# A DeltaNet recurrence with a SwiGLU FFN: one stream of units, inversions by pairs, and a fixed order

## The chip, the cores and the metric

The kernel runs on one core of a Trainium2 chip. The metric is the device time of one execution in microseconds (us), the median of several runs. A core has five engines that run side by side, each with its own queue of instructions: TensorE (matmuls, PE in the profile; its weight loads are PEld), VectorE (DVE), ScalarE (ACT), GpSimd (POOL) and SyncE (SP), which here only starts DMA transfers. TensorE writes to PSUM, and VectorE and ScalarE move results from there to SBUF.

## The reference: what is computed

Two layers follow each other. The first is a DeltaNet: for each of 4 batches and 8 heads a state of 48x48 is carried over 768 positions.

```python
k_n = k / (np.linalg.norm(k, axis=-1, keepdims=True) + 1e-06)
for t in range(S):                                   # S = 768
    y[:, :, t] = einsum('bhd,bhde->bhe', q[:, :, t], state)
    v_old = einsum('bhde,bhd->bhe', state, k_n[:, :, t])
    state += beta[:, :, t, None, None] * einsum('bhd,bhe->bhde', k_n[:, :, t], v[:, :, t] - v_old)
```

The second is an FFN on the 3072 tokens of width 384 (8 heads x 48), with 1536 inner columns:

```python
xn = x / sqrt(mean(x * x) + 1e-06) * rms_g
out = (silu(xn @ w_gate) * (xn @ w_val)) @ w_out
```

The kernel doesn't walk over positions. It cuts the 768 positions into 6 chunks of 128 and calls one chunk of one batch a **unit**; there are 24, and unit n is chunk n // 4 of batch n % 4. Inside a unit the positions depend on each other through a triangular system, which is inverted in blocks of 32 positions (and the blocks are then joined by matmuls). Between chunks only the state of a batch is passed on. All data are float32; the weights arrive as 64-bit floats and are converted on the chip.

## The kernel before

A unit goes through these steps. `prepare` transposes q and k on TensorE, forms all products of keys and queries (`score`), and writes the 32x32 diagonal blocks out to DRAM, from where they come back with one block on each partition (`gather`):

```python
def gather(n):
    c, b = divmod(n, B)                      # B = 4
    ...
    for a in range(NBLK):
        dma(out=gds[c][...], in_=gp[b][W * a : W * (a + 1), :, o : o + W])
    if b == B - 1:
        nc.sync.dma_start(out=gblk, in_=gds.pop(c))

def prepare(n):
    norm_k(n, square_k(n, nc.scalar))
    yield 4
    transpose(n, qpad[n % 2], Q0)
    ...
    yield 3
    transpose(n, kpad[n % NK], K0)
    yield 2
    score(n, crossed((0, slice(0, 3)), (1, slice(1, 4))), both)
    yield 1
    gather(n)
```

With 4 units x 8 heads x 4 blocks, the 128 blocks of a whole chunk lie on the 128 partitions and are inverted together, in 31 steps of two VectorE instructions:

```python
def invert(c, dt):
    clear_ttb()
    scale_beta(c)
    turn_beta(c)                             # p_nb on TensorE, nbeta on VectorE
    for b in range(B):
        scale_v(B * c + b)
    yield dt
    for i in range(W - 1):                   # W = 32
        ...
        nc.vector.scalar_tensor_tensor(out=tmp, in0=gblk[...], scalar=nbeta[:, i : i + 1],
                                       in1=ttb[...], op0=ALU.mult, op1=ALU.mult)
        nc.vector.tensor_tensor(out=to, in0=to, in1=tmp, op=ALU.add)
        yield dt
    nc.sync.dma_start(out=td, in_=ttb)
    nc.vector.tensor_tensor(out=gblk, in0=ttb..., in1=nbeta..., op=ALU.mult)
    nc.sync.dma_start(out=nd, in_=gblk)
    ...                                      # td and nd are read back as tt[b] and ne
```

The recurrence of a chunk is a small pipeline over its 4 units. Stage `corner` joins the 32-blocks of one unit (p_v) and of the one before it (p_w); `inner` forms z, u and x of three neighbouring units in one loop of small matmuls; `outer` applies the state of one unit (p_k), forms the output of another (p_y) and updates its state (p_s):

```python
for s in range(-3, B + 2):                   # once per chunk, from chunk 1 on
    inner(s, s - 1, s + 1)                   # z of s, u of s-1, x of s+1, if they exist
    yield dt
    outer(s + 1, s - 1)
    yield dt
    if s + 2 in units or s + 3 in units:
        corner(s + 3, s + 2)
    if s - 1 in units:
        ys[s - 1] = scale(*ys[s - 1])
    if s - 2 in units:
        transpose_y(B * c + s - 2, ys.pop(s - 2))      # p_xt, then xt for the FFN
    yield dt
```

The FFN takes 256 tokens at a time, in 12 tiles f of 128 inner columns:

```python
for f in range(f0, f1):
    for i in range(2):                       # gate, value
        ... # matmuls p_gv[:, i] <- wgv_sb, xt
        yield 1
    nc.scalar.activation(out=sil, in_=p_gv[:, 0], func=ACTF.Silu)
    nc.vector.tensor_tensor(out=h_f, in0=sil, in1=p_gv[:, 1], op=ALU.mult)
    if last is not None:
        leave(f - 1, last)                   # matmuls p_o <- h_f, wo_sb
        yield 1
    last = h_f
```

All parts are generators on one plan. `at(time, part)` starts a part, a `yield dt` puts its next piece dt later, and the pieces are written to the program by their plan time. A unit of plan time stands for one stretch of FFN matmuls. Up to plan time 60 the program is issued just as it is written; after that a scheduler of the framework may move instructions.

```python
CYC = 3 * FT * B // 2                        # 72
for c in range(1, NCH):
    t0 = CYC * c
    for b in range(B):
        at((8 if c == 1 else t0 - 76) + 4.5 * b, prepare(B * c + b))
    at(35 if c == 1 else t0 - 49, invert(c, 0.62))
    at(*((57, recur(c, 0.7)) if c == 1 else (t0 - 25, recur(c, 1.2))))
    for g in range(B // 2):
        at(t0 + CYC // 2 * g, ffn(B // 2 * c + g, 0, FT))
with tc.manual_schedule():
    first = recur(0, 1.2, begin())
    ...
    run_plan(60)
run_plan()
```

Of the kernel before, what the change touches and what calls it, by code (L numbers as in the profile page):

```python
# [21 lines left out]
W = 32  # L22
# [6 lines left out]
def kernel(  # L29
# [36 lines left out]
    NK = B + 1  # L66
# [20 lines left out]
    g_sb = const.tile([128, KT], FP32, name="g_sb")  # L87

# [22 lines left out]
    vraw, later = {}, []  # L111

# [136 lines left out]
    def weights():  # L249
# [37 lines left out]
        bits_pool.close()  # L287

# [36 lines left out]
    def scale_beta(c):  # L325
        nrm = norms[c]
        nc.vector.tensor_scalar_add(nrm, nrm, 1e-6)
        krec = work.tile([128, BH], FP32, name="krec", bufs=1)
        nc.vector.reciprocal(krec, nrm)
        for i in range(2):  # L330
            nc.vector.tensor_tensor(out=beta_t[:, c], in0=beta_t[:, c], in1=krec, op=ALU.mult)

    def turn_beta(c):
        p_nb = ps_delta([128, W], "p_nb")
        for a in range(NBLK):
            wa = slice(W * a, W * (a + 1))
            nc.tensor.matmul(p_nb[wa], beta_t[wa, c], ident[wa, wa], skip_group_check=True)
        nc.vector.tensor_scalar(out=nbeta, in0=p_nb, scalar1=-1.0, scalar2=None, op0=ALU.mult)

# [10 lines left out]
    def transpose(n, pad, place):  # L350
# [11 lines left out]
        nc.scalar.copy(kqt[n % B][:, :, place::2], p_t)  # L362


    def score(n, groups, evacuate):
        b = n % B
# [31 lines left out]
    def gather(n):  # L398
        c, b = divmod(n, B)
        dma = nc.scalar.dma_start  # L400
        if b == 0:
            gds[c] = dram.tile([128, W, W], FP32, name="gd")
        for a in range(NBLK):
            o = diagonal(a)
            dma(
                out=gds[c][a * BH + b * H : a * BH + (b + 1) * H].rearrange("h r j -> r h j"),
                in_=gp[b][W * a : W * (a + 1), :, o : o + W],
            )
        if b == B - 1:
            nc.sync.dma_start(out=gblk, in_=gds.pop(c))  # L410


    def gather_two(n):
        if n == 0:
            gds[0] = dram.tile([128, W, W], FP32, name="gd")
# [15 lines left out]
    def prepare(n):  # L431
        norm_k(n, square_k(n, nc.scalar))
        yield 4
        transpose(n, qpad[n % 2], Q0)
        if n + 2 < NU:
            load_q(n + 2)
        yield 3
        transpose(n, kpad[n % NK], K0)
        yield 2
        score(n, crossed((0, slice(0, 3)), (1, slice(1, 4))), both)  # L440
        yield 1
        gather(n)
# [45 lines left out]
    def clear_ttb():  # L488
        nc.gpsimd.memset(ttb, 0.0)  # L489
        nc.gpsimd.memset(ttb.rearrange("p j i -> p (j i)")[:, 0 : W * W : W + 1], 1.0)  # L490


    def invert_halves():
# [25 lines left out]
        td = dram.tile([128, W, W], FP32, name="td")  # L519
        nc.sync.dma_start(out=td, in_=ttb)  # L520

        nd = dram.tile([128, W, W], FP32, name="nd")
# [21 lines left out]
    def invert(c, dt):  # L544
        clear_ttb()
        scale_beta(c)
        turn_beta(c)
        for b in range(B):
            scale_v(B * c + b)
        yield dt  # L550
        for i in range(W - 1):
            n = W - 1 - i
            shape = [128, i + 1, n]
            tmp_b = work.tile([128, W * W // 4], FP32, name="tmp")
            tmp = tmp_b[:, 0 : n * (i + 1)].rearrange("p (k j) -> p k j", j=n)
            nc.vector.scalar_tensor_tensor(  # L556
                out=tmp,
                in0=gblk[:, i, None, i + 1 :].to_broadcast(shape),
                scalar=nbeta[:, i : i + 1],
                in1=ttb[:, 0 : i + 1, i : i + 1].to_broadcast(shape),  # L560
# [3 lines left out]
            to = ttb[:, 0 : i + 1, i + 1 :]  # L564
            nc.vector.tensor_tensor(out=to, in0=to, in1=tmp, op=ALU.add)  # L565
            yield dt
        td = dram.tile([128, W, W], FP32, name="td")
        nc.sync.dma_start(out=td, in_=ttb)

        nd = dram.tile([128, W, W], FP32, name="nd")  # L570
        nc.vector.tensor_tensor(
            out=gblk,
            in0=ttb.rearrange("p s m -> p m s"),
            in1=nbeta[:, :, None].to_broadcast([128, W, W]),
            op=ALU.mult,
        )
        nc.sync.dma_start(out=nd, in_=gblk)
        for b in range(B):
            for a in range(NBLK):
                o = W * (a % 2)  # L580
                nc.sync.dma_start(
                    out=tt[b][W * a : W * (a + 1), :, o : o + W],
                    in_=td[a * BH + b * H : a * BH + (b + 1) * H].rearrange("h r j -> r h j"),
                )
            for a in (0, 2):
                nc.sync.dma_start(
                    out=ne[W * a : W * (a + 1), b * H : (b + 1) * H],
                    in_=nd[a * BH + b * H : a * BH + (b + 1) * H].rearrange("h r j -> r h j"),
                )
        yield dt  # L590

    xts = {}
# [9 lines left out]
    def recur(c, dt, inverses=None):  # L604
        units = range(B)
        vss, x2s, p_zs, us = {}, {}, {}, {}

        def over_d(b, p):
            return beta_t[p, c, b * H : (b + 1) * H, None].to_broadcast([HC, H, D])


        def corner(b_v, b_w):
            p_v = ps_delta([128, H, W], "p_v") if b_v in units else None
            p_w = ps_delta([128, H, W], "p_w") if b_w in units else None
            for h in range(H):
                for a in (0, 2):
                    wa, wb = (slice(W * x, W * (x + 1)) for x in (a, a + 1))
                    if b_v in units:
                        o = diagonal(a)
                        nc.tensor.matmul(  # L620
                            p_v[wa, h],
                            gp[b_v][wb, h, o : o + W],
                            tt[b_v][wb, h, W:HC],
                            skip_group_check=True,
                        )
                    if b_w in units:
                        nc.tensor.matmul(  # L627
                            p_w[wa, h],
                            left(b_w)[wa, h, 0:W],
                            vss[b_w][wa, h],  # L630
                            skip_group_check=True,
                        )
            if b_v in units:
                if c == 0:
                    turn(b_v)
                vss[b_v] = work.tile([128, H, W], FP32, name="vs")
            for a in (0, 2):
                wa = slice(W * a, W * (a + 1))
                if b_v in units:
                    nc.scalar.copy(vss[b_v][wa], p_v[wa])  # L640
                if b_w in units:
                    nc.scalar.copy(tt[b_w][wa, :, W:HC], p_w[wa])


        def left(b):
            if c == 0:
                return ne_2[:, b % 2 * H : (b % 2 + 1) * H]
            return ne[:, b * H : (b + 1) * H]


        def turn(b):
            turned = work.tile([128, W * W // 4], FP32, name="tmp").rearrange(
                "p (h j) -> p h j", j=W
            )
            nc.vector.transpose(out=turned, in_=tt[b][:, :, 0:W])
            for a in (0, 2):
                wa = slice(W * a, W * (a + 1))
                nc.vector.scalar_tensor_tensor(
                    out=left(b)[wa, :, 0:W],
                    in0=turned[wa],  # L660
                    scalar=-1.0,
                    in1=beta_t[wa, c, b * H : (b + 1) * H, None].to_broadcast([W, H, W]),
                    op0=ALU.mult,
                    op1=ALU.mult,
# [4 lines left out]
        def halves(b):  # L669
            p_v = ps_delta([128, H, 2, SW], "p_vh")  # L670
            for h in range(H):
                for p, place in ((lo, K0), (hi, K1)):
                    nc.tensor.matmul(
                        p_v[p, h],
                        gp[b][p, h, HC * place : HC * (place + 1)],
                        tt[b][p, h].rearrange("p (x j) -> p x j", x=2)[:, :, SW:W],
                        skip_group_check=True,
                    )
            v_h = work.tile([128, H, W], FP32, name="vs")
            nc.scalar.copy(v_h.rearrange("p h (x j) -> p h x j", x=2), p_v)  # L680
            yield
            p_w = ps_delta([128, H, 2, SW], "p_wh")
            for h in range(H):
                for p in (lo, hi):
                    nc.tensor.matmul(
                        p_w[p, h].rearrange("p x j -> p (x j)"),
                        left(b)[p, h],
                        v_h[p, h],
                        skip_group_check=True,
                    )  # L690
            for a in range(NBLK):
                up, at = slice(W * a, W * a + SW), W * (a % 2) + SW
                to = tt[b][up, :, at : at + SW]
                if b % 2:
                    nc.scalar.copy(to, p_w[up, :, a % 2])
                else:
                    nc.vector.tensor_copy(out=to, in_=p_w[up, :, a % 2])
            yield


        def outer(b_k, b_y):
            if b_k in units and c > 0:
                p_k = ps_delta([128, H, D], "p_k")
                product(p_k, kqt[b_k], (K0, K1), state[b_k], True)
                r = vraw[B * c + b_k]
# [397 lines left out]
```

## Time and profile before

| what | value |
|---|---|
| time, median of 3 runs | 864.64 us (863.49 to 866.26) |
| span of the profiled execution | 866.4 us |
| TensorE busy | 832.2 us, 96% |
| VectorE busy | 411.9 us, 48% |
| ScalarE busy | 251.7 us, 29% |
| GpSimd busy | 107.0 us, 12% |
| mean granted TensorE clock | 0.982 |
| first FFN matmul | at 65.7 us |
| period of a chunk in the steady part | 132.0 us (564.2 to 696.3 us, the same point of two chunks) |

The profile names each group of instructions by the line of the kernel, the engine, and out<-in by the names of the program. The matmuls are pipelined, so the time of a stage is best read from the start of one group to the start of the next in the timeline. The FFN's lines are 958 (p_gv) and 945 (p_o); line 969 is h_f, the product that p_o needs. Lines 556 and 565 are the two instructions of an inversion's step. Lines 771, 780 and 789 are z, u and x in `inner`, 753 p_k and the state's part of p_y, 373 the scores, 387 their masks, 405 and 410 the two transfers of the gather. In the slices of the page each digit is the busy share of 1/40 of the span, in tenths.

### The profile page before, as it was taken

The page shows a single profiled execution, that of the slowest core. Times are in us where ns is not written, and L with a number is a line of the kernel's source. Part 1 is how long each engine was busy: PE and PEld are TensorE (multiplying, and loading weights), DVE is VectorE, ACT ScalarE, POOL GpSimd, SP SyncE. Part 2 cuts the span into 40 slices and gives each one's busy share as a digit, 9 for nine tenths or more (in the row PEclk, how much of TensorE's full clock was granted, in tenths as well). Part 3 has the DMA queues.
Part 4 walks back from the last instruction along what each step waited for, and adds up shares of the span by engine and source line. Part 5 has one row for each costly group of instructions (what it writes and reads, how often), then busy time and mean ns, then how long its engine had stood idle before and what let it go on. Part 6 is the DMA issues. An engine that isn't in the chain of part 4 may idle for free.

```text
span 866.4 us, 20251 instructions
## 1 busy us (share of the span) xinstructions
PE 832.2 (96%) x8640; PEld 638.7 (74%) x8640; DVE 411.9 (48%) x1000; ACT 251.7 (29%) x655; POOL 107.0 (12%) x146
## 2 busy tenths in 40 slices
PE   7898979689999999999999999999999999999998
PEld 6576757467887777877777887777777777777776
DVE  7869969791443761343661442671333581220100
ACT  5344446003334113244113244112334112220101
POOL 6012433100230000230000230000130000000000
PEclk9969999899999999999999999999999999999999
DMA  8846345104221131221121222122121122000000
GB/s 152 231 99 211 121 122 144 31 24 90 48 62 34 32 84 28 48 62 32 31 83 32 43 61 37 31 78 38 39 57 19 31 71 35 2 20 0 19 1 18
DMA packets 152058, 52.01 MB, mean 60 GB/s; under 512 B 143616, under 2 KB 146688, under 8 KB 151968
## 3 DMA queue, kind: packets, MB, share of 16 engines
q1 hardware_dynamic: 124816, 36.95, 18.5%
q0 software_dynamic: 2080, 10.23, 3.5%
q10 hardware_dynamic: 25072, 3.54, 2.3%
q8 instruction: 68, 1.11, 0.5%
q14 instruction: 22, 0.18, 0.1%
HBM read 36.54 MB, written 14.16 MB: 59 GB/s over the span
## 4 chain that ended last, share of the span: by engine, by line
PE 79%; DVE 15%; issue 2%; ACT 2%; DMA 1%; POOL 1%; SPq 0%; DVEq 0%; ACTq 0%; POOLq 0%
PE p_gv L958 38%; PE p_o L945 18%; DVE tmp L556 4%; DVE ttb L565 3%; PE p_g L373 3%; PE p_y L715 3%; PE p_z L771 2%; PE p_t L357 2%; PE p_k L753 2%; PE p_y L753 2%; PE p_z L780 1%; PE p_x L789 1%; PE p_v L620 1%; PE p_w L627 1%; DVE h_f L969 1%
## 5 line engine op out<-in xcount | busy, mean ns | idle before, releaser
L958 PE MATMUL p_gv<-xt,wgv_sb 128*128 128x256 f32 x1728 | 416.1, 386 | 1.3 <-DVE xt L929 0.7
L958 PEld LDWEIGHTS p_gv<-xt,wgv_sb 128*128 128x128 f32 x1728 | 321.5, 191 | 66.0 <-issue 4.3
L945 PE MATMUL p_o<-wo_sb,h_f 128*128 128x384 f32 x576 | 217.7, 502 | 9.0 <-DVE h_f L969 9.0
L969 DVE TENSOR_TENSOR h_f<-sil,p_gv 128x256 f32<-128x256 f32 x144 | 60.2, 418 | 247.3 <-ACT sil L967 247.2
L967 ACT ACTIVATE sil<-p_gv 128x256 f32<-128x256 f32 x144 | 55.1, 383 | 335.8 <-PE p_gv L958 314.4
L945 PEld LDWEIGHTS p_o<-wo_sb,h_f 128*128 128x128 f32 x576 | 105.0, 192 | 61.2 <-DVE h_f L969 13.8
L556 DVE SCALAR_TENSOR_TENSOR tmp<-gblk,nbeta,ttb 128x31 f32<-128x31 f32 (+15 forms) x155 | 62.7, 405 | 4.7
L387 DVE TENSOR_TENSOR gp<-p_g,mask 64x128 f32<-64x128 f32 (+1 forms) x160 | 37.9, 277 | 43.2 <-ACT gp L383 38.7
L565 DVE TENSOR_TENSOR ttb<-ttb,tmp 128x31 f32<-128x31 f32 (+15 forms) x155 | 53.0, 342 | 4.9
L320 POOL TENSOR_TENSOR knrm<-ksum,half 128x8 f32<-128x8 f32 x24 | 41.8, 1741 | 71.0 <-DVE ksum L319 70.8
L914 POOL TENSOR_SCALAR ms<-ms 128x1 f32<-128x1 f32 x24 | 5.3, 221 | 312.0 <-ACT y L906 311.7
L362 ACT COPY kqt<-p_t 128x512 f32<-128x512 f32 x48 | 28.1, 585 | 24.9 <-PE p_t L357 24.2
L489 POOL MEMSET ttb<- 128x1024 f32 x6 | 5.7, 954 | 228.9 <-DMA td<-ttb 228.9
L771 PEld LDWEIGHTS p_z<-v_raw,tt 64*64 64x64 f32 x768 | 26.0, 142 | 9.2 <-issue 7.2
L373 PE MATMUL p_g<-kqt 64*64 64x192 f32 x640 | 31.7, 330 | 0.9 <-ACT gp L383 0.9
L640 ACT COPY vs<-p_v 32x256 f32<-32x256 f32 x48 | 17.4, 362 | 44.4 <-PE p_w L627 23.2
L780 PE MATMUL p_z<-u,x 64*64 64x48 f32 x384 | 28.8, 227 | 0.7 <-DVE u L801 0.6
L789 PE MATMUL p_x<-tt,gp 64*64 64x64 f32 x384 | 29.0, 229 | 0.2 <-issue 0.2
L771 PE MATMUL p_z<-v_raw,tt 64*64 64x48 f32 x768 | 29.2, 227 | 0.0
L373 PEld LDWEIGHTS p_g<-kqt 64*64 64x64 f32 x640 | 23.1, 132 | 8.1 <-issue 5.3
L715 PE MATMUL p_y<-u,gp 128*64 128x48 f32 x768 | 27.6, 228 | 0.0
L780 PEld LDWEIGHTS p_z<-u,x 64*64 64x64 f32 x384 | 25.7, 142 | 2.4 <-issue 1.3
(117 smaller groups left out, 784.1 us busy)
## 6 DMA issues: line engine op xcount, KB each, us to landing
kpad<-in_k_dram SPq DMA_DIRECT2D x24, 192.0 KB, 2.9
qpad<-in_q_dram SPq DMA_DIRECT2D x24, 192.0 KB, 2.9
v_raw<-in_v_dram SPq DMA_DIRECT2D x24, 192.0 KB, 2.9
out_dram<-o_sb SPq DMA_DIRECT2D x24, 192.0 KB, 1.9
gblk<-gd SPq DMA_DIRECT2D x6, 512.0 KB, 3.3
td<-ttb SPq DMA_DIRECT2D x6, 512.0 KB, 2.6
raw<-in_moe_w_val_dram POOLq DMA_DIRECT2D x8, 384.0 KB, 4.3
raw<-in_moe_w_out_dram POOLq DMA_DIRECT2D x8, 384.0 KB, 4.3
```

Of the source, the lines that this page charges most:

```text
L320: nc.gpsimd.tensor_tensor(out=norms[c][:, b * H : (b + 1) * H], in0=ksum, in1=half, op=ALU.pow)
L373: nc.tensor.matmul(to, pair[d, K1 if i else K0], pair[d, places], skip_group_check=True)
L387: nc.vector.tensor_tensor(out=to[p, :, place], in0=p_g[p, :, place], in1=mask[p, i, None].to_broadcast([p.stop, 2, HC]), op=ALU.mult,)
L556: nc.vector.scalar_tensor_tensor(out=tmp, in0=gblk[:, i, None, i + 1 :].to_broadcast(shape), scalar=nbeta[:, i : i + 1], in1=ttb[:, 0 : i ...
L565: nc.vector.tensor_tensor(out=to, in0=to, in1=tmp, op=ALU.add)
L715: nc.tensor.matmul(p_y[p, h], gp[b_y][:, h, HC * place : HC * (place + 1)], u[:, h], start=(c == 0 and h == 0), stop=True, skip_group_chec ...
L771: nc.tensor.matmul(p_zs[b_z][p, h], tt[b_z][p, h], r[p, h], start=(h == 0), stop=(p is lo), skip_group_check=True,)
L780: nc.tensor.matmul(p_zs[b_u][hi, h], x2s[b_u][:, h], us[b_u][lo, h], start=False, stop=True, skip_group_check=True,)
L945: nc.tensor.matmul(p_o[i], h_f[:, i * C : (i + 1) * C], wo_sb[:, f], start=(f == f0), stop=(f == f1 - 1),)
L958: nc.tensor.matmul(p_gv[:, i], wgv_sb[:, i * KT + t, f * 128 : (f + 1) * 128], xt[:, t], start=(t == 0), stop=(t == KT - 1),)
L967: nc.scalar.activation(out=sil, in_=p_gv[:, 0], func=ACTF.Silu)
L969: nc.vector.tensor_tensor(out=h_f, in0=sil, in1=p_gv[:, 1], op=ALU.mult)
```

## The change

The ends of the recurrence between chunks go: from unit 4 on, one slot per unit takes the next unit in, so that `corner` and `inner` always work on full neighbours, across the border of a chunk too. For that, units can't be inverted by chunks any more: from chunk 2 on they are inverted in pairs, each on 64 of the 128 partitions, in time for their slots. Keys, kqt and gp get two more buffers where needed (they lie where the weights were converted before). u of the second half gets a PSUM tile of its own and is added on VectorE. `scale_beta` moves from the start of the inversion to the end of the last `prepare`. The Silu is written right after the gate and value matmuls. The whole program is issued in the order in which the plan writes it; no scheduler moves anything.

The diff, cut to its core (cuts marked by a line of dots):

```diff
-    NK = B + 1
+    NK = B + 2
...
+    def place_of(n):
+        return n % B if n < 2 * B else (n - B) % NK
...
+    def turn_two(g):
+        c, own = betas(g, 2)
+        p = group(g, 2)
+        apart = work.tile([128, NBLK, 2 * H], FP32, name="apart", bufs=1)
+        nc.vector.tensor_tensor(out=apart, in0=beta_t[...], in1=in_block[...], op=ALU.mult)
+        p_nb = ps_delta([128, W], "p_nb")
+        nc.tensor.matmul(p_nb[p], apart.rearrange("p a h -> p (a h)"), of_block, skip_group_check=True)
+        nc.vector.tensor_scalar(out=nbeta[p], in0=p_nb[p], scalar1=-1.0, scalar2=None, op0=ALU.mult)
...
-        if b == B - 1:
-            nc.sync.dma_start(out=gblk, in_=gds.pop(c))
+        if i == size - 1:
+            nc.sync.dma_start(out=gblk[group(n // size, size)], in_=gds.pop(n // size))
...
-    def prepare(n):
+    def prepare(n, size, dts):
...
-        yield 1
-        gather(n)
+        yield dts[3]
+        gather(n, size)
+        if n % size == size - 1:
+            scale_beta(n // size, size)
...
-    def invert(c, dt):
-        clear_ttb()
-        scale_beta(c)
-        turn_beta(c)
-        for b in range(B):
-            scale_v(B * c + b)
+    def invert(g, size, dt):
+        p = group(g, size)
+        np = size * NBLK * H
+        clear_ttb(p)
+        if size == B:
+            turn_beta(g)
+            for n in range(B * g, B * (g + 1)):
+                scale_v(n)
+        else:
+            turn_two(g)
         yield dt
         for i in range(W - 1):
             n = W - 1 - i
-            shape = [128, i + 1, n]
+            shape = [np, i + 1, n]
...
+        if have(n_u):
+            u = us[n_u][hi]
...
+                nc.vector.tensor_tensor(out=tmp_b[hi], in0=p_u[hi], in1=over_d(n_u, hi), op=ALU.mult)
+                nc.vector.tensor_tensor(out=u, in0=u, in1=tmp_b[hi], op=ALU.add)
...
-        for s in range(-3, B + 2):
-            inner(s, s - 1, s + 1)
...
+    def slot(j, dts):
+        v, z, y = (n if B <= n < NU else None for n in (j, j - 1, j - 2))
+        if have(v) and v >= 2 * B:
+            scale_v(v)
+        if have(v) or have(z):
+            corner(v, z)
+        yield dts[0]
+        inner(z, y, z)
+        yield dts[1]
+        outer(v, y)
+        reload()
+        yield dts[2]
+        if have(y):
+            scaled = scale(*ys.pop(y))
+            yield dts[3]
+            transpose_y(y, scaled)
...
+                if i == 1:
+                    sil = work.tile([128, TOK], FP32, name="sil")
+                    nc.scalar.activation(out=sil, in_=p_gv[:, 0], func=ACTF.Silu)
                 yield 1
-            sil = work.tile([128, TOK], FP32, name="sil")
-            nc.scalar.activation(out=sil, in_=p_gv[:, 0], func=ACTF.Silu)
...
-    for c in range(1, NCH):
-        t0 = CYC * c
-        for b in range(B):
-            at((8 if c == 1 else t0 - 76) + 4.5 * b, prepare(B * c + b))
-        at(35 if c == 1 else t0 - 49, invert(c, 0.62))
-        at(*((57, recur(c, 0.7)) if c == 1 else (t0 - 25, recur(c, 1.2))))
+    for b in range(B):
+        at(8 + 4.5 * b, prepare(B + b, B, (4, 3, 2, 1)))
+    at(35, invert(1, B, 0.62))
+    for g in range(B // 2):
+        at(72 + 36 * g, ffn(B // 2 + g, 0, FT))
+    begins = {B: 57, B + 1: 59.7, B + 2: 62.4, B + 3: 65, 2 * B: 89, 2 * B + 1: 96}
+    for j in range(B, NU + 2):
+        begin_j = begins.get(j, 18 * (j - 3) - 15)
+        at(begin_j, slot(j, (1, 1, 1, 1) if j < 2 * B else (2, 2, 2, 1.5)))
+    for g in range(B, NU // 2):
+        if g == B:
+            start = 62
+        elif g == B + 1:
+            start = 79
+        else:
+            start = (102 if g == B + 2 else 18 * (2 * g - 6) - 15) + 8.6
+        for x in range(2):
+            at(start + 3.6 * x, prepare(2 * g + x, 2, (1.4, 1.2, 1.4, 1)))
+        at(start + 9.2, invert(g, 2, 0.5))
+        at(36 * g, ffn(g, 0, FT))
     with tc.manual_schedule():
...
-        run_plan(60)
-    run_plan()
+        run_plan()
```

## The prediction

> **What bounds the kernel now.** I read the page first (busy shares and the 40 slices), then TensorE's timeline in one steady chunk and in the first 200 us, then all engines around one inversion, then VectorE's groups by shape.
>
> The page's busy shares and slices:
>
> ```profile
> PE 832.2 (96%) x8640; PEld 638.7 (74%) x8640; DVE 411.9 (48%) x1000; ACT 251.7 (29%) x655; POOL 107.0 (12%) x146
> ...
> PE   7898979689999999999999999999999999999998
> ...
> DVE  7869969791443761343661442671333581220100
> ```
>
> One slice is 21.7 us. TensorE shows 9 in every slice from 195 us to the end; its holes lie before. VectorE averages a half, but the average hides peaks: a pair of slices with 6 to 8 returns once per chunk (around 290, 420, 560 and 690 us), and that is the inversion. So after about 200 us the time is a sum of TensorE work, and whatever makes TensorE wait is added to the end: the last gate/value and output matmuls of the FFN must all run in any case.
>
> How TensorE's stages cost, from its timeline (start, length, instruction):
>
> ```profile
> 593.07 1.14 PE L789 MATMUL p_x<-tt,gp 64*64 64x64 f32 x16
> 594.14 1.56 PE L945 MATMUL p_o<-wo_sb,h_f 128*128 128x384 f32 x4
> ...
> 608.45 0.26 PE L771 MATMUL p_z<-v_raw,tt 64*64 64x48 f32 x2
> 608.46 0.25 PE L780 MATMUL p_z<-u,x 64*64 64x48 f32 x1
> 608.47 0.27 PE L789 MATMUL p_x<-tt,gp 64*64 64x64 f32 x1
> ...
> 609.54 1.56 PE L958 MATMUL p_gv<-xt,wgv_sb 128*128 128x256 f32 x6
> ```
>
> An `inner` stage with only the x of one unit takes 593.07 to 594.14, 1.07 us; one with z, u and x together takes 608.45 to 609.54, 1.09 us. A half-empty stage costs as much as a full one.
>
> Around an inversion, all engines:
>
> ```profile
> 672.72 1.53 PE L373 MATMUL p_g<-kqt 64*64 64x192 f32 x32
> ...
> 675.63 1.81 ACTq L405 DMA_DIRECT2D gd<-gp  x4
> ...
> 678.79 0.34 SPq L410 DMA_DIRECT2D gblk<-gd  x1
> ...
> 683.39 0.24 DVE L556 SCALAR_TENSOR_TENSOR tmp<-gblk,nbeta,ttb 128x31 f32<-128x31 f32 x1
> ```
>
> The last score stage ends at 674.18 (next start). The blocks go out at 675.63, are fetched back at 678.79 and land 3.2 us later: 7.8 us from score to `gblk`. The first inversion step comes 1.4 us after that, so today nothing waits for it.
>
> And what TensorE suffers when VectorE falls behind:
>
> ```profile
> 564.17 1.56 PE L945 MATMUL p_o<-wo_sb,h_f 128*128 128x384 f32 x4 [0.73 <-DVE h_f L969]
> ```
> ```profile
> 190.00 2.65 PE L945 MATMUL p_o<-wo_sb,h_f 128*128 128x384 f32 x4 [2.68 <-DVE h_f L969]
> 192.45 5.98 PE L958 MATMUL p_gv<-xt,wgv_sb 128*128 128x256 f32 x24
> ```
>
> The steps of the inversion stand in VectorE's queue between the FFN's products h_f. Today this costs 0.7 us per chunk.
>
> **What the Trainium skill says.** "PSUM — Partial Sum Buffer", Engine vs sequencer instructions: VectorE's queue is strict FIFO, and matmuls keep program order. The trace agrees: the 0.73 us above is TensorE standing at one p_o with later matmuls behind it. "VectorE: DVE Perf Modes", on why tensor_reduce can't reduce along the partition axis: each partition is its own lane and the data stream along the free dimension. So 64 partitions cost what 128 do; the trace agrees (mask product 64x128 282 ns, 128x128 273 ns). "TensorE: Matmul & The Clock Gate", Part 1: after an idle window of about 3.4 us the array runs at half clock until it has been busy as long. Here the 2.68 us wait is followed by four p_o in 2.45 us instead of 1.29 us.
>
> **The change, part by part.**
>
> *Merged stages (gain).* Before, each of five chunks runs its own ramp: 6 `inner` and 5 `corner` stages for 4 units. As one stream, 20 units take 21 of each. That removes 9 `inner` x 1.08 = 9.7 us and 4 `corner` x 0.65 = 2.6 us, and with them 13 changes between small and large matmuls at about 0.1 us (six p_gv take 1.40 us after a small stage, 1.29 us otherwise). Sum: 14 us. The early activation and the old waits for h_f after 200 us (0.7 us per chunk and a little) are worth 3 us.
>
> *Pairs inverted (more VectorE work).* Chunks 2 to 5 need 8 inversions of 64 partitions instead of 4 of 128. One is 31 steps of two instructions. Summing the means by shape, 12.5 us for the first kind and 10.6 us for the second, plus about 0.04 us gap each (694.48 to 694.94 for a 0.42 us instruction), gives 25.3 us, and the last product gblk 1.94 us: 27.3 us. Four more are 109 us of VectorE. The separate u costs two more instructions per unit, about 0.5 us net.
>
> *Written order (takes a choice away).* Steps follow each other by 0.5 plan units instead of 0.62. Three units are one FFN tile f of 3.88 us (12 p_gv in 2.59, 4 p_o in 1.29), so six steps (5.4 to 5.9 us) and h_f (0.34) stand against 3.88 us of TensorE work. And the inversion is written 0.6 units after the gather of the pair's second unit, against 3.5 units before. I read the changed order: VectorE has beta, `apart`, `nbeta`, two steps, then h_f; the first step waits for the DMA of gblk.
>
> *One steady pair.* T is the end of the second unit's score. TensorE, in written order up to the p_o that needs the sixth h_f after it: FFN 24.6 us (6.5 tiles of p_gv x 2.59, 6 p_o x 1.29), p_nb 0.2, two `corner` 1.4, `inner` 1.1, p_k, p_y and p_s 2.9, p_xt 0.3, changes of shape about 2: **32.6 us**. VectorE: it cannot start a step before gblk has landed; I take 7.4 us for half the bytes (7.8 for the whole, of which 3.2 us is the fetch). Then 27.3 for the inversion, six h_f 2.0, and of the recurrence slot that falls into it u 1.6, r 0.56, state 0.7, xt 0.56: **40.1 us**. The difference, **7.5 us**, is TensorE's wait; it cannot be dodged, because p_o stands in its queue. Outside these 40 us VectorE has some 12 us of work per pair against 29 us of TensorE, so it recovers and the next pair starts clean. Five pairs (units 14 to 23) have this pattern: 38 us.
>
> *The three early pairs.* Units 8, 9: VectorE 7.4 + 36 us (two units' masks and norms fall into it) before the next pair's `apart`, which TensorE's p_nb needs; TensorE's own work to there is 31 us. Wait 13 us. Units 10, 11: 37 us of VectorE and some waits against 35 us: 4 us. Units 12, 13: as a steady pair, 8 us. Sum 25 us.
>
> *The start.* Up to the first chunk's inversions and the FFN below 190 us, TensorE's and VectorE's orders are almost unchanged. scale_beta moves ahead in VectorE's queue, but the conversion of the weights it overtakes still stands before the next h_f, so the hole at 155 to 160 us (4.8 us for p_nb) only changes its name. The first `corner` of chunk 1 now stands one p_o earlier and waits for tt (the first eight reads are issued by 198.4 us in the timeline and take 2.2 us by the list of transfers, so they land at about 200.6 us, while the p_gv before it end at 198.3): +2 us.
>
> Sum: 864.6 - 14 - 3 + 38 + 25 + 2 = 912.6; I say 912 us.
>
> **Rivals.**
> 1. *TensorE stays the bound, VectorE's doubling is hidden.* For: VectorE is at 57.4 of 132 us in a steady chunk; with 55 more and the u products it would be under 90%. The old inversion ran beside the FFN nearly free. Against: that one took steps at 0.62 and already touched the limit (0.73 us). If the wait for gblk and the pace were both absorbed, the time would be 864.6 - 17 + 2 = 850 us.
> 2. *Only the pace counts, the wait for gblk is hidden* (the DMA lands by the time VectorE gets there, since masks and beta come first and take some 4 us). Then a pair costs about 4.5 us, and the eight about 40 us: 890 us.
> 3. *The waits also halve the clock.* For: the pair at 190.00. Against: a slower TensorE right after a wait mostly eats the next wait, since VectorE sets the pace there. Should it not, each pair adds up to 1.7 us: 925 us.
>
> **Range and chances.** The mechanism rests on in-order queues and counted durations, so I give rival 1 under a fifth. My uncertain terms are the landing of gblk (2 us per pair, 16 us) and the early pairs (10 us). Range 880 to 934 us. Faster by over 2% (below 847): 0.08; within 2%: 0.11; slower (above 882): 0.81.
>
> **What would show it.** Right: VectorE near 520 to 540 us busy; the inversion's two lines at 279 instructions each with the same means; each pair's first step idle 2 to 3 us for the DMA gd to gblk; TensorE waiting in total 55 to 75 us after 200 us, named h_f, p_nb or u; a steady pair 70 to 72 us long instead of 66 (half of a chunk's 132 us); 21 full `inner` stages at 1.09 us. Wrong: a pair at 63 to 64 us with no TensorE wait (rival 1), steps on 64 partitions that are shorter than on 128, or gblk in place before VectorE asks (rival 2).

## The result and the profile after

The changed kernel takes 919.48 us (median of 4 runs, 914.78 to 922.55) against 865.0 us of the kernel before on the same chip. The ratio is 1.0626, with a 95% interval of 1.0577 to 1.0675: 6.3% slower, as predicted (912 us, range 880 to 934).

The page of the changed kernel: busy time with instruction counts, the 40 slices (23 us each), the engines' shares of the chain that ended last, and three groups (count | busy us, mean ns | idle us before them and what ended it).

```profile
PE 834.8 (91%) x8624; PEld 635.1 (69%) x8624; DVE 520.8 (57%) x1303; ACT 248.7 (27%) x655; POOL 113.4 (12%) x156
...
PE   7888897989988888888989899899899899999998
...
DVE  7869879844595945939538637727825922121110
...
PE 42%; DVE 29%; DMA 5%; ACT 3%; issue 3%; SPq 1%; ACTq 1%; DVEq 0%
...
L1019 PE MATMUL p_o<-wo_sb,h_f 128*128 128x384 f32 x576 | 224.5, 515 | 36.3 <-DVE h_f L1044 36.2
...
L612 DVE SCALAR_TENSOR_TENSOR tmp<-gblk,nbeta,ttb 64x112 f32<-64x112 f32 (+19 forms) x279 | 113.0, 405 | 47.3 <-DMA gblk<-gd 37.7
L621 DVE TENSOR_TENSOR ttb<-ttb,tmp 64x112 f32<-64x112 f32 (+19 forms) x279 | 96.4, 345 | 9.6
```

TensorE's row of nines (slice 10 to the end before) now has eights from slice 12 to 19 and then an 8 at regular distances, and VectorE has eight peaks after slice 10 instead of four. VectorE gained 109 us (411.9 to 520.8), most of it in the two lines of the inversion: they have 279 instructions each, nine times 31 (eight pairs and chunk 1), against five times 31. Of the chain VectorE holds 29% (15% before). For comparison, two groups of the kernel before:

```profile
L945 PE MATMUL p_o<-wo_sb,h_f 128*128 128x384 f32 x576 | 217.7, 502 | 9.0 <-DVE h_f L969 9.0
L556 DVE SCALAR_TENSOR_TENSOR tmp<-gblk,nbeta,ttb 128x31 f32<-128x31 f32 (+15 forms) x155 | 62.7, 405 | 4.7
```

The waits of the changed kernel, in us in total, times, longest:

```profile
DVE tmp L612 <- DMA gblk<-gd: 37.7, 8, 8.5
PE p_o L1019 <- DVE h_f L1044: 36.2, 33, 2.9
...
PE p_nb L378 <- DVE apart L371: 17.5, 8, 3.1
```

Before, TensorE waited 9.0 us in all for h_f and 4.8 us for p_nb. One steady pair in the timeline of all engines (start, length, instruction, idle time before it):

```profile
546.48 1.53 PE L416 MATMUL p_g<-kqt 64*64 64x192 f32 x32
...
549.39 1.81 ACTq L448 DMA_DIRECT2D gd<-gp  x4
...
551.31 0.23 DVE L371 TENSOR_TENSOR apart<-beta_t,in_block 128x64 f32<-128x64 f32 x1
551.69 0.27 PE L378 MATMUL p_nb<-of_block,apart 128*64 128x32 f32 x2 [2.18 <-DVE apart L371]
...
552.64 0.47 SPq L453 DMA_DIRECT2D gblk<-gd  x1
...
556.44 0.25 DVE L612 SCALAR_TENSOR_TENSOR tmp<-gblk,nbeta,ttb 64x31 f32<-64x31 f32 x1 [4.25 <-DMA gblk<-gd]
```

The score ends at T = 547.94 (the start of the next FFN matmul). TensorE stands 2.18 us at p_nb, because `apart` is written behind the masks, an h_f and `scale_beta` in VectorE's queue; VectorE then stands 4.25 us for the blocks, which it gets 8.5 us after T. The same pair on TensorE alone, to the p_nb of the next:

```profile
552.59 2.88 PE L1032 MATMUL p_gv<-xt,wgv_sb 128*128 128x256 f32 x6
555.26 1.87 PE L1019 MATMUL p_o<-wo_sb,h_f 128*128 128x384 f32 x4
...
578.70 1.70 PE L1019 MATMUL p_o<-wo_sb,h_f 128*128 128x384 f32 x4 [2.68 <-DVE h_f L1044]
580.20 4.34 PE L1032 MATMUL p_gv<-xt,wgv_sb 128*128 128x256 f32 x12
...
589.83 1.56 PE L1019 MATMUL p_o<-wo_sb,h_f 128*128 128x384 f32 x4 [0.52 <-DVE h_f L1044]
...
624.33 0.37 PE L378 MATMUL p_nb<-of_block,apart 128*64 128x32 f32 x2 [2.18 <-DVE apart L371]
```

After both long holes the matmuls run slower for a while: six p_gv take 2.88 us and twelve 4.34 us, where 1.56 and 2.86 us are usual (552.59 against 587.74, 580.20 against 558.15). This pair is 72.64 us long (551.69 to 624.33), the next 70.81; half of a chunk before was 66.0.

### The profile page after: what moved, and what is told of

Read it like the earlier page. It is cut to its first block, busy times and chain, and to the rows that moved or that the text cites. A ratio compares the mean times of both kernels' runs of the same rounds, so it can differ in the third digit from the quotient of the medians.

```text
span 918.0 us, 20509 instructions
## 1 busy us (share of the span) xinstructions
PE 834.8 (91%) x8624; PEld 635.1 (69%) x8624; DVE 520.8 (57%) x1303; ACT 248.7 (27%) x655; POOL 113.4 (12%) x156
## 4 chain that ended last, share of the span: by engine, by line
PE 42%; DVE 29%; DMA 5%; ACT 3%; issue 3%; SPq 1%; ACTq 1%; DVEq 0%
PE p_gv L1032 21%; PE p_o L1019 12%; DVE tmp L612 11%; DVE ttb L621 10%; DMA gblk<-gd 3%; DVE h_f L1044 2%; PE p_g L416 2%; ACT gp L425 1%; DVE gblk L627 1%; PE p_y L775 1%; ACT gp L426 1%; PE p_k L813 1%; DMA gd<-gp 1%; PE p_t L400 1%; PE p_y L813 1%
## 5 line engine op out<-in xcount | busy, mean ns | idle before, releaser
L1032 PE MATMUL p_gv<-xt,wgv_sb 128*128 128x256 f32 x1728 | 424.4, 394 | 1.3 <-DVE xt L1003 0.7
L1032 PEld LDWEIGHTS p_gv<-xt,wgv_sb 128*128 128x128 f32 x1728 | 331.4, 196 | 68.8 <-issue 5.2
L1019 PE MATMUL p_o<-wo_sb,h_f 128*128 128x384 f32 x576 | 224.5, 515 | 36.3 <-DVE h_f L1044 36.2
L1019 PEld LDWEIGHTS p_o<-wo_sb,h_f 128*128 128x128 f32 x576 | 107.1, 197 | 98.7 <-DVE h_f L1044 50.2
L612 DVE SCALAR_TENSOR_TENSOR tmp<-gblk,nbeta,ttb 64x112 f32<-64x112 f32 (+19 forms) x279 | 113.0, 405 | 47.3 <-DMA gblk<-gd 37.7
L621 DVE TENSOR_TENSOR ttb<-ttb,tmp 64x112 f32<-64x112 f32 (+19 forms) x279 | 96.4, 345 | 9.6
L835 PEld LDWEIGHTS p_z<-v_raw,tt 64*64 64x64 f32 x768 | 25.7, 142 | 10.6 <-issue 9.5
L335 DVE TENSOR_REDUCE ksum<-ksq 128x8 f32<-128x384 f32 x24 | 13.2, 548 | 32.1 <-ACT ksq L325 31.5
L877 ACT ACTIVATE gp<-p_x 64x512 f32<-64x512 f32 x24 | 14.2, 590 | 47.7 <-PE p_x L853 47.7
L853 PEld LDWEIGHTS p_x<-tt,gp 64*64 64x64 f32 x384 | 25.6, 142 | 0.3 <-issue 0.3
```

The lines of the kernel that those rows point to most:

```text
L612: nc.vector.scalar_tensor_tensor(out=tmp, in0=gblk[p, i, None, i + 1 :].to_broadcast(shape), scalar=nbeta[p, i : i + 1], in1=ttb[p, 0 : i ...
L835: nc.tensor.matmul(p_z[p, h], tt[n_z % B][p, h], r[p, h], start=(h == 0), stop=(p is lo or n_z >= B), skip_group_check=True,)
L853: nc.tensor.matmul(p_x[lo, h], gp[place_of(n_x)][hi, h, HC * K0 : HC * (K0 + 1)], tt[n_x % B][hi, h], skip_group_check=True,)
L1019: nc.tensor.matmul(p_o[i], h_f[:, i * C : (i + 1) * C], wo_sb[:, f], start=(f == f0), stop=(f == f1 - 1),)
L1032: nc.tensor.matmul(p_gv[:, i], wgv_sb[:, i * KT + t, f * 128 : (f + 1) * 128], xt[:, t], start=(t == 0), stop=(t == KT - 1),)
```

## The experiments

All are timed against the kernel before on the same chip, so ratios are compared; 0.01 is 8.7 us. The expectations name these theories. **Q**: the loss is where the written order puts VectorE's work, so another place for the same work wins it back. **V**: VectorE has simply too much to do, and no place helps. **D**: only the wait for the transfer of the blocks costs. **W** (from the run with one step on): the written order as such costs, whatever the places in it.

**1. The last five inversions begin later, or go slower, or both.** The fixed start of an inversion's steps after `prepare` is 9.2 plan units, their pace 0.5.

```diff
-        at(start + 9.2, invert(g, 2, 0.5))
+        at(start + (14 if g > 6 else 9.2), invert(g, 2, 0.5))                               # e1_later
+        at(start + 9.2, invert(g, 2, 0.75 if g > 6 else 0.5))                               # e2_slower
+        at(start + (13 if g > 6 else 9.2), invert(g, 2, 0.75 if g > 6 else 0.5))            # e3_both
```

> In the last five pairs (units 14 to 23) the inversion, with its turn of beta, starts 4.8 plan units later (14 instead of 9.2 after the pair's start); its pace stays at 0.5. By then gblk has landed. Theory Q (VectorE's queue sets the pace: the wait for gblk and the dense steps each cost): the waits for gblk and for p_nb go in these five pairs, but the dense steps now meet the second slot of the period, so some 3 to 4 us of TensorE's wait per pair stay. 7.5 us per pair were lost, 3.5 to 4 come back: 898 to 903 us. Rival D (the DMA wait alone): all 7.5 us come back, 880 to 885 us. Rival V (VectorE's added work costs wherever it stands): 915 to 922 us.

> In the last five pairs the steps of the inversion follow each other by 0.75 plan units instead of 0.5; it starts where it did, so gblk is still awaited. Theory Q: the waits for h_f in the dense part go, the wait for p_nb (2.2 us per pair) and the slow clock after it stay. About 4 us per pair come back: 896 to 902 us. Rival D: nothing comes back, 915 to 922 us. Rival V: 915 to 922 us.

> Later (13 instead of 9.2 plan units after the pair's start) and slower (0.75) together in the last five pairs. Theory Q: 7.5 us per pair come back, the period of a pair falls from 71.4 us to about 64: 880 to 886 us. Rival D: 880 to 885 as for the later start alone. Rival V: 915 to 922 us.

| run | us | ratio [95%] | won back against the change |
|---|---|---|---|
| later | 895.49 | 1.0339 [1.0304, 1.0373] | 2.9% = 25 us |
| slower | 888.62 | 1.0257 [1.0231, 1.0283] | 3.7% = 32 us |
| both | 877.26 | 1.0109 [1.0070, 1.0147] | 5.2% = 45 us |

All three came out 3 to 7 us below the ranges that Q gave; V's 915 to 922 us is out for all three, and D is out too, since the slower pace wins 32 us back while the blocks come as late as before, and the later start alone doesn't reach 885 us. The two single edits add up to 57 us, more than both together: they overlap. What stays in each shows how. The later start, VectorE's waits in the first line and TensorE's timeline in the others:

```profile
DVE tmp L612 <- DMA gblk<-gd: 16.5, 3, 8.8
```
```profile
431.20 1.56 PE L1019 MATMUL p_o<-wo_sb,h_f 128*128 128x384 f32 x4 [1.69 <-DVE h_f L1044]
437.32 1.56 PE L1019 MATMUL p_o<-wo_sb,h_f 128*128 128x384 f32 x4 [1.09 <-DVE h_f L1044]
...
565.36 1.56 PE L1019 MATMUL p_o<-wo_sb,h_f 128*128 128x384 f32 x4 [1.67 <-DVE h_f L1044]
```

The blocks are waited for only by the three early pairs now, and p_nb by none of the last five; what stays in the last five pairs is mostly the pace, h_f behind six steps. The slower pace, in the same two views:

```profile
DVE tmp L612 <- DMA gblk<-gd: 38.0, 8, 8.9
```
```profile
474.72 0.27 PE L378 MATMUL p_nb<-of_block,apart 128*64 128x32 f32 x2 [2.18 <-DVE apart L371]
475.63 1.56 PE L1032 MATMUL p_gv<-xt,wgv_sb 128*128 128x256 f32 x6
...
540.16 0.27 PE L378 MATMUL p_nb<-of_block,apart 128*64 128x32 f32 x2 [2.18 <-DVE apart L371]
541.06 2.37 PE L1032 MATMUL p_gv<-xt,wgv_sb 128*128 128x256 f32 x6
543.23 2.38 PE L1019 MATMUL p_o<-wo_sb,h_f 128*128 128x384 f32 x4
...
607.29 0.27 PE L378 MATMUL p_nb<-of_block,apart 128*64 128x32 f32 x2 [2.18 <-DVE apart L371]
```

VectorE waits as long for the blocks as in the changed kernel (38.0 against 37.7 us), and in the last five pairs TensorE no longer feels it: only p_nb is left. So here the wait for the blocks costs something only together with the fast pace. With nothing but the 2.18 us at p_nb a pair takes 65.44 us (474.72 to 540.16) where the clock stays up and 67.13 us (540.16 to 607.29) where it drops.

**2. The work of the steps taken away.** First the loop was cut to one step, its places in the plan with it:

```diff
-        for i in range(W - 1):
+        for i in range(W - 1 if size == B else 1):
```

> All eight inversions by pairs make one step instead of 31 (the result is then not the reference's); transfers, products and everything else stay. It measures what the change would bring without the work of the pairs' steps. Theory Q: all of the waits after 200 us go except those for gblk, which shrink because nothing is queued behind; the floor is 864.6 minus 14 to 17 us plus the 2 us at the start, and up to 2 us per pair for p_nb: 850 to 866 us. If the merged stages brought nothing, it would be 865 to 880 us.

It took 937.7 us (1.0823 [1.0797, 1.0850]) instead of the expected 850 to 866, slower than the change itself: this experiment failed. Without the steps' places the read of tt moves up in the written order, and TensorE meets it on its way (12 such waits at p_z, 59.9 us in all; this is one):

```profile
407.52 0.42 PE L835 MATMUL p_z<-v_raw,tt 64*64 64x48 f32 x2 [9.83 <-DMA tt<-td]
```

Hence the repeat, with 30 of 31 steps left out and their places kept:

```diff
         for i in range(W - 1):
+            if size < B and i > 0:
+                yield dt
+                continue
```

> The eight inversions by pairs issue the first of their 31 steps and leave the other 30 out (so the output isn't the reference's); all places in the plan are kept, the transfers stay where they were. (In the run before, the missing steps had let the transfers move up in the order, into the reads of the units before; that is undone here.) Theory Q: only the waits that don't come from the steps are left, those of p_nb (2.2 us per steady pair) with the slow clock behind them and some early ones: 862 to 875 us. Rival V (VectorE's bandwidth as such) says the same. Rival W (the written order itself costs): 890 us and more.

868.08 us, 1.0014 [0.9997, 1.0031], inside what was expected. The steps' presence in this order costs 1.0626 - 1.0014 = 6.1% = 53 us. The waits that are left are mostly at p_nb: 2.18 us in each of the last five pairs, 2.12, 2.55 and 1.38 in the early ones.

**3. Is the written order in itself a loss?** The kernel before, all of it in written order:

```diff
-        run_plan(60)
-    run_plan()
+        run_plan()
```

> The kernel before, with the whole program in written order: one part of the change alone. Theory Q: the written order is no loss in itself, since the old plan leaves 3.5 units between gather and inversion and paces the steps at 0.62: 858 to 875 us. Rival W: a large part of the 55 us that the change lost, 885 us and more.

866.47 us, 0.9993 [0.9972, 1.0014]. It isn't, with the old plan, and W falls. The other way round, the changed kernel with the scheduler from plan time 60 on:

```diff
-        run_plan()
+        run_plan(60)
+    run_plan()
```

> The changed kernel, but from plan time 60 on the framework's scheduler may move instructions, as in the kernel before. Theory Q: it may move a step behind an h_f, but VectorE's work and the late gblk stay: 895 to 922 us. Rival W: the loss came from the written order, so 865 to 880 us.

886.68 us (median of all four), 1.0216 [1.0185, 1.0248], between the two expectations, so neither is borne out. (The profiled execution was a disturbed, slower one: the ratio leaves it out, and only the order is read from its trace.) In the order that the scheduler made, `apart` stands ahead of the masks, three h_f stand between it and the first step, and four steps stand before most h_f and up to seven before some, instead of six. It moves the work the same way as experiment 1: 4.1% = 36 us came from the order being fixed in this form. Which of these moves won it was not tested.

**4. The same work in better places.** From experiment 1 and the waits of the early pairs, all eight inversions get new starts and paces, the `prepare` of the three early pairs new starts too, and the slots of units 8 to 13 new times (dots inside a line stand for text left out):

```diff
-    begins = {B: 57, ..., 2 * B: 89, 2 * B + 1: 96}
+    begins = {B: 57, ...}
+    begins.update({2 * B: 93, 2 * B + 1: 100, 2 * B + 2: 123, 2 * B + 3: 133, 2 * B + 4: 152, 2 * B + 5: 169})
+    early = {B: (55, 12.5, 0.65), B + 1: (86, 12.5, 0.6), B + 2: (112, 12.5, 0.7)}
...
+        start, wait, pace = early.get(g, (18 * (2 * g - 6) - 15 + 8.6, 13, 0.75))
...
-        at(start + 9.2, invert(g, 2, 0.5))
+        at(start + wait, invert(g, 2, pace))
```

> The changed kernel with a new plan and nothing else: in the last five pairs the inversion 13 plan units after the pair's start at 0.75; the three early pairs start at 55, 86 and 112 instead of 62, 79 and 110.6, with their inversion 12.5 units later at 0.65, 0.6 and 0.7; slots 8 to 13 at 93, 100, 123, 133, 152, 169. Theory Q: the early waits (about 24 us of holes between 200 and 400 us, and the slow clock after them) go too: 848 to 860 us, so the merged stages show at last. Rival V: no better than 875 us.

855.65 us, 0.9880 [0.9837, 0.9923]. TensorE's timeline still had a wait that one number mends, the slot of unit 12 ahead of its tt:

```profile
388.13 0.22 PE L682 MATMUL p_v<-tt,gp 32*32 32x32 f32 x2 [2.22 <-DMA tt<-td]
...
389.40 0.21 PE L682 MATMUL p_v<-tt,gp 32*32 32x32 f32 x1 [0.93 <-DMA tt<-td]
```

```diff
-    ... 2 * B + 4: 152, ...
+    ... 2 * B + 4: 155.5, ...
```

> The replanned order with the slot of unit 12 begun 3.5 plan units (4.5 us) later, so that its first corner no longer meets tt on its way (2.22 + 0.93 us of TensorE in the replanned run). Theory Q (the loss sits in the placement of waits, each wait is time): those two waits go and nothing else moves, 851 to 854 us against 855.6. If a wait only moves on to the next slot (unit 13 close behind it): 855 to 857.

850.84 us, 0.9811 [0.9797, 0.9825], at the lower end of the 851 to 854 expected: 1.9% faster than the kernel before and some 70 us below the change, with the change's instructions. The page of this run:

```profile
PE 810.8 (95%) x8624; PEld 626.4 (74%) x8624; DVE 523.3 (62%) x1303; ACT 248.2 (29%) x655; POOL 112.4 (13%) x156
...
PE   7898979789999989999999999999999999999998
...
DVE  7868978892596686886956847846847831211110
```

VectorE does as much as in the change (523.3 us, 1303 instructions), and TensorE's nines are back. V falls for good: VectorE's load is no bound.

**5. What merging is worth, with the inversion out of the way.** The plan of the 855.65 us run (slot of unit 12 still early) with the pairs' steps left out (the edit of experiment 2), and the kernel before in written order with the steps of chunks 2 to 5 left out:

> The replanned order with 30 of the 31 steps of every pair's inversion left out, their places in the plan kept: the merged stream without the pairs' VectorE work. Theory M (merged stages are worth the 14 us of the prediction): 845 to 851 us, and 10 to 16 us under the next run, in which the chunks keep their own ramps and leave the same steps out. Rival R (what the replanned order gains comes from waits it removes and not from merging): the two lie within 4 us of each other. If the pairs' VectorE work is still felt in the replanned order, this run is more than 6 us under it.

> The kernel before in written order, with 30 of the 31 steps of the inversions of chunks 2 to 5 left out, places kept: only the h_f waits of some 0.7 us per chunk can go. 860 to 865 us. Under M 10 to 16 us above the merged floor, under R within 4 us of it.

The second of these left nothing out: its edit asked for the wrong variable, and VectorE kept 1000 instructions. So its 865.72 us (0.9988 [0.9973, 1.0003]) only measures the written order once more. Mended:

```diff
         for i in range(W - 1):
+            if c > 1 and i > 0:
+                yield dt
+                continue
```

> The kernel before in written order, now really with 30 of the 31 steps of the inversions of chunks 2 to 5 left out (the run above it left nothing out: VectorE still had 1000 instructions), places kept. Theory M (merging itself is worth the 14 us): 860 to 865 us, 10 to 16 us above the merged floor of 849.9, VectorE at 760 instructions. Rival R (the gain of the replanned order is removed waits): within 4 us of the merged floor, 846 to 854 us.

Merged: 849.88 us, 0.9801 [0.9787, 0.9814]. With chunks: 857.2 us, 0.9883 [0.9851, 0.9915]. The gap is 0.8%, 7 us: neither M's 10 to 16 nor R's at most 4, and the second run lies outside the range of both. The busy times and the timelines tell why. Merged:

```profile
PE 808.1 (96%) x8624; PEld 624.4 (74%) x8624; DVE 348.3 (41%) x823; ACT 248.6 (29%) x655; POOL 119.2 (14%) x156
```
```profile
447.74 0.24 PE L378 MATMUL p_nb<-of_block,apart 128*64 128x32 f32 x1
...
574.38 0.24 PE L378 MATMUL p_nb<-of_block,apart 128*64 128x32 f32 x1
```

With chunks:

```profile
PE 822.9 (96%) x8640; PEld 634.6 (74%) x8640; DVE 327.5 (38%) x760; ACT 248.2 (29%) x655; POOL 104.8 (12%) x146
```
```profile
411.50 0.26 PE L337 MATMUL p_nb<-ident,beta_t 32*32 32x32 f32 x8 [0.33 <-DVE beta_t L331]
541.80 0.26 PE L337 MATMUL p_nb<-ident,beta_t 32*32 32x32 f32 x8 [0.33 <-DVE beta_t L331]
```

TensorE is busy 14.8 us less, and four units take 126.64 us (574.38 - 447.74) instead of 130.30: 3.66 us per chunk, 14.6 in four. That is M's gain. But TensorE idles 37.2 us in the merged run (span 845.3) against 33.0 (span 855.9), so some 4 us of it go into waits, the largest for tt at the slot of unit 12 (2.56 us). The rest of the gap between profiles and medians is within the scatter of single runs (847.1 to 849.9 and 851.8 to 858.4).

Against the same plan with its steps (0.9880), the merged run gains 0.8%, some 7 us and uncertain by 4: this is what the pairs' steps still cost there. It isn't lost in the last five pairs. After 400 us TensorE waits for h_f just as little with all steps (first line, the 850.84 us run) as without them (second line, the merged run):

```profile
PE p_o L1019 <- DVE h_f L1044: 0.7, 4, 0.2
PE p_o L1022 <- DVE h_f L1047: 0.7, 4, 0.2
```

## Why the prediction was right, step by step

The time was 919.5 instead of 912 us, and the chain of causes is the one foretold: VectorE's added steps, packed between two h_f behind late blocks, hold TensorE up in order. It differs in the points below.

| step | predicted, us | measured, us | from |
|---|---|---|---|
| merged stages | -14 | -14.8 | TensorE busy, experiment 5 |
| old waits for h_f | -3 | -9 | 0.9993 to 0.9883 when the steps go |
| other waits in the merged order | 0 | +7 | what is left to the -17 of the merged run (0.9801) |
| last five pairs | +38 | +45 | 1.0626 to 1.0109 |
| three early pairs, with slots and start | +25 and +2 | +26 | 1.0109 to 0.9811 |

The measured column counts from 865.0. The fastest run (0.9811) lies 1 us above the merged run (0.9801): it has the steps, and the slot of unit 12 in a better place. 865 - 17 + 1 + 26 + 45 = 920. A difference of two such ratios is uncertain by some 5 us. In part the total came out close by luck: the second row is wrong by 6 us and the third by 7 us the other way.

**VectorE's work.** 520.8 us were foretold as 520 to 540, and 279 instructions in each of the two lines; a step on 64 partitions takes what one on 128 takes (first step 0.25 us here, 0.24 us before). Right, but for one sum: 12.5 + 10.6 + 62 x 0.04 is 25.6 us for the steps, not 25.3.

**The steady pair.** "7.5 us is TensorE's wait" and "70 to 72 us long": the five pairs' p_nb stand at 408.27, 480.86, 551.69, 624.33 and 695.14, 71.7 us apart. Without waits a pair takes 63.3 us (half of 126.64; the prediction had 63 to 64). So the excess is 8.4 us, not 7.5. Its parts:
- The blocks came at T + 8.5 (T + 8.3 in the next pair), not at T + 7.4; VectorE idled 4.25 us for them instead of "2 to 3 us". The prediction took something off for half the bytes; the whole of before had needed 7.8. VectorE's chain of 40.1 us became 41.9 us (T to the p_o at 589.83, which needs the sixth h_f after the first steps) and in the next pair 40.1 us (620.59 to 660.64):

```profile
660.64 1.56 PE L1019 MATMUL p_o<-wo_sb,h_f 128*128 128x384 f32 x4 [0.23 <-DVE h_f L1044]
```

- TensorE's own 32.6 us were right. From the last p_o that waits to the next T it takes 30.76 us in both pairs, 0.17 of it idle; 63.3 less 30.6 leaves 32.7 us.
- Of TensorE's lost time 5.5 to 5.6 us a pair are idle (2.18 at p_nb, the rest at h_f); its total after 200 us was about 50 us, below the 55 to 75 expected. The rest is half clock. In the stretch from 551.7 to 560 us the granted clock is 0.79, from 578 to 590 it is 0.86: (1 - 0.79) x 8.3 + (1 - 0.86) x 12 = 3.4 us. The next pair has one such stretch (0.78 over 7.7 us, 1.7 us). But the third rival is not borne out by it: the last p_o of each stretch still waits for its h_f (0.52 and 0.23 us), so VectorE's chain sets the length, as the prediction argued, and its 41.89 against 40.05 us is the whole difference between the two pairs. Why the chain is longer in one of them stays open; pairs lie on the upper and the lower 64 partitions in turn.

**"It cannot be dodged, because p_o stands in its queue."** That step failed as a statement on the change, though not on this order. The slower pace alone dodges the h_f waits with VectorE idling for the blocks as before, and in the order of the 850.84 us run the steps of the last five pairs cost no h_f wait at all (0.7 us with and without them). Queues in order make the wait follow from the places, and the places were free.

**p_nb.** The steady pair was given 0.2 us for p_nb and no wait; only the early pairs were to wait there. All eight wait, 1.4 to 3.1 us. While VectorE sets the pair's length, this wait only comes in place of one at h_f; it becomes a cost of its own when the pace is mended (experiments 1 and 2).

**The early pairs.** Their sum was about right, its parts and the place of the wait were not. The p_nb that was to wait 13 us waited 3.09 us. From p_nb to p_nb (238.5, 278.5, 354.1 and 408.3 us) TensorE idled 7.1, 9.2 and 6.8 us, and lost 3.6 and 3.8 us to the clock in the first two (0.91 over 40.0 us, 0.95 over 75.6): 11, 13 and 7 us against 13, 4 and 8, spread over p_t, p_nb and many h_f.

**The start.** The first corner waited 0.46 + 0.81 us for tt (2 foretold). The hole before 160 us did change its name: before, p_o 1.84 us for h_f and p_nb 4.79 us; after, p_o 1.37, p_nb 0.93 and p_o 2.90 us.

**The old h_f waits.** In the kernel before they are 0.7 us per chunk, as read. In written order they are 1.5 us (6.2 us in four, after 200 us), and taking the steps out there is worth 2.0: a chunk takes 132.28 us (p_nb at 280.03 and 412.31) with the steps and 130.30 without. What makes up the other half microsecond stays open.

**Rival 1's number** (850 us, everything hidden) was reached, by another plan: 850.84. For the change as it stood it was wrong. **Rival 2** was wrong for the change, whose blocks were never in place in time; experiment 1 gives it half right, as the wait for them costs no h_f wait at a slower pace. The third row of the table was not foreseen; 4 us of it are the idle time named in experiment 5, and the rest is not settled.

## What to carry to other kernels

When a change multiplies the work of an engine that is not the bound, count how much of it the written order puts between two instructions that the bounding engine needs: here six steps (5.4 us and more) between two h_f against 3.88 us of matmuls, behind late blocks, cost 8 us a pair, and four steps with a later start cost nothing in the last five pairs. The wait for the transfer hurt here only because the work behind it was packed tighter than the other engine's pace, so spread it first, and start it later if there is slack before its consumer. And before giving a good merge up for its measured loss, take the added work out with its places kept: the floor (here 2% under the kernel before) says what there is to win, and a new order with all the work in it, whether the work or its place is at fault.

## What the runs showed that was not expected

The same hole of 2.18 us was followed by a drop of the clock in some pairs and not in others. In the slower-pace run, the stretches after p_nb (length, busy time of TensorE, its weight loads, VectorE, ScalarE, GpSimd, then the granted clock) are:

```profile
474.70:482.00 7.30, 7.28 (x152) 5.88 (x152) 2.69 (x9) 2.23 (x6) 0.00 (x0) 1.00 0.19 45
540.20:547.50 7.30, 7.30 (x144) 5.37 (x145) 2.25 (x8) 2.23 (x6) 0.00 (x0) 0.77 0.17 43
```

0.23 x 7.3 = 1.7 us, and that is the difference between its pairs (65.44 and 67.13 us). In its five pairs the clock is 0.77, 1.00, 0.77, 1.00 and 1.00, in the run with one step the same; in the changed kernel it is 0.77 in all five, as here:

```profile
480.90:488.20 7.30, 7.30 (x145) 5.73 (x146) 2.92 (x11) 2.23 (x6) 0.00 (x0) 0.77 0.15 45
```

So which half of the partitions a pair lies on does not decide it. The Trainium skill, "TensorE: Matmul & The Clock Gate", Part 1, has the clock fall after an idle window of about 3.4 us that runs free of the kernel. A free-running window could fit a drop after some holes and not after others; but the hole of 2.18 us is shorter than the page's window, and here the measurement decides. No run varied the phase, so the cause of the alternation stays open. Where TensorE sets the pace, such a hole counts as 2.2 to 3.9 us here.
